# One six-step group becomes two four-step groups, and the whole order of work is written anew

## The chip, the cores and the metric

The kernel runs on one core of a Trainium2 chip. Times are device microseconds of one execution; the time before is the median of three runs. The five engines are TensorE (PE, with its weight loads shown as PEld), VectorE (DVE), ScalarE (ACT), GpSimd (POOL) and SyncE (SP), each with a queue of its own that it works through in the order written; DMAs are issued from the queues of SP, ACT and POOL.

## The reference

A causal convolution over time with three taps and a dilation of 2, a gate, and a projection. With `x` of 2 x 16000 x 256, `w` of 3 x 256 x 512 and `w_o` of 256 x 256, all bf16:

```python
h = x[t] @ w[0] + x[t-2] @ w[1] + x[t-4] @ w[2]      # zero where the time is below 0
f, g = h[..., :256], h[..., 256:]
out = (tanh(f) * sigmoid(g)) @ w_o
```

## The kernel before

**Groups.** Time is cut into groups, listed per sequence in `GROUPS`. A group of kind A has `R` = 256 rows of six consecutive steps (1,536 steps), a group of kind B has `R` rows of four steps. Rows lie on the free axis and channels on the partitions: a transposing DMA from SP loads a group as the tile `xt`. The first group, P160, is computed directly with 320-column matmuls. Since the dilation is 2, even and odd steps don't mix, and a row of six steps is three outputs for each parity, a row of four steps two.

**Fewer products.** Instead of three products per output, an A group makes its three outputs from five products, and a B group its two outputs from four. The operands of the products are sums and differences of shifted views of `xt`; the weights are sums of the taps (`wa`, `wm`, `wp`, and the taps themselves). Each product of a block is two matmuls (two halves of the 256 channels) of 512 columns when R = 256, and of 2R columns in general. A block is one quarter of the 512 output channels of a group, so a group has four blocks, and `ORDER` says in which order blocks are computed.

**The operands.** An A group needs `u1` (for the first product, with `wa`) and four more: `rp` = f + u1, `rm` = e + u1/3, `r0` = u0 - u1/2, `ri` = u2 + 2 u1. The parts `u0`, `u1`, `u2`, `e`, `f` are read from `xt`, by VectorE (whole tiles of 1,024 elements per partition) or by GpSimd (quarters of 256). `u3`, `uh`, `ud` are `u1` times 1/3, -1/2 and 2, made by VectorE. The four sums are mostly made by accumulating DMAs: GpSimd's queue issues a DMA that adds `u1`, `u3`, `uh` or `ud` onto the tile that holds `f`, `e`, `u0` or `u2`, 256 KB each. A B group needs `m`, `p`, `d0`, `d3`, each one difference or sum of views of `xt`.

**The outputs.** The first product goes to PSUM bank `b`; ScalarE copies it to SBUF as `ss`. VectorE combines `ss` and `b` into bank `a`; for A groups a copy `hh` (VectorE or ScalarE) and a second combination `yy` give the middle output. ScalarE applies tanh or sigmoid to `b`, `yy` and `a`. VectorE multiplies the halves (the gate, tile `zz`), TensorE multiplies by `wo_sb` into `o_ps`, ScalarE or VectorE evicts it to `osb`, and SP stores it.

**What sets the order.** `PLAN` is a list of tokens, written by hand or by a planner and executed in that order at build time; each token appends instructions to the queue of its engine. No engine reorders its own queue, and between the queues there are only semaphores for real dependences. The tokens that matter here:

- `F M L Z I`: one product of the next block (first, `rm`, `rp`, `r0`, `ri`; in B blocks F, L, Z, I use `m`, `p`, `d0`, `d3`).
- `P`, `H`, `R`: matmuls of the projection. `c`, `k`, `b`, `y`, `a`, `e`: ScalarE's copies, activations and evictions. `A`, `h`, `Y`, `g`, `v`: VectorE's combinations, gate and evictions.
- `u0.3`: the part u0 of the fourth A group (they count from 0), whole, on VectorE. `u0.3q7`: a quarter of it on GpSimd, held until the VectorE instruction that stands seven places before the latest one is done. `r0.3d`: the accumulating DMA that makes r0 of that group. `rm.2` without the d: the same sum on VectorE.
- `wa.7q2`: a piece of the combined weights on GpSimd.
- `x`: load of the next group on SP. `s9`: a store on SP. A load that stands behind a store on SP waits until that store's evictions are done.

There are four buffers for six-step tiles (the first of them used by group 0) and four for four-step tiles. Groups are numbered in the order of `GROUPS`: 0 is P160, 1 to 8 are the A groups and 9 to 11 the B groups of the first sequence, 12 onward are the second sequence.

The lines that the profile names: L167 load, L325 accumulating DMA, L328 and L330 operands, L359 products, L379 direct convolution, L390 copy `ss`, L393 VectorE's combinations, L403 copy `hh` on ScalarE, L441 activations, L460 gate, L478 projection, L487 and L495 evictions, L504 store.

Of the kernel before, what the change touches and what calls it, by code (L numbers as in the profile page):

```python
# [22 lines left out]
L G c Z g I b f.0 P a L A e0 wa.4q1 P wa.1q1 A F I u1.0 c Z u2.0 a x L b u3.0 Z m.2 I wa.15q1 b F A a wa.12q12 P F  # L23
uh.0 c g Z e1 L e.0 b I e2 A P rm.0d c x F d3.2 a rp.0d L p.2 e3 Z c d0.2 I b P A wa.14q1 a L u2.1 wa.9q27 e4 F A Z
c wa.0q30 I g b wa.8q2 Z a L ud.0 wa.5q10 b I A F wa.2q13 a u1.1 F ri.0d c Z u0.0 c I u3.1 b L r0.0d u0.1 a P A s0 L
wa.11q1 e5 F g wa.13q1 Z c A I wa.10q16 b M f.1 a Z u1.2 k0 P rp.1d b ud.1 F uh.1 L e6 e.1 u0.2q1 F c s3 A I c M
u3.2 u0.2q18 a P Y k1 M rm.1d e.2 e7 Z ri.1d g k2 I L b r0.1d g P a A F e8 uh.2 L u1.3q42 c Y s4 P y s2 A M u1.3q24
x e9 Z h3 u1.3q49 y P Y I b u0.2q39 L v10 a u1.3q47 F Y y u0.2q7 Z c A I r0.2d y P g Z b M u3.3 b F ud.2 k4 f.2 I c
F ud.3 a L u2.2 x c M A P k5 rm.2 P e.3q1 a L Y e11 M A e12 e.3q32 I k6 Z uh.3 e.3q4 Y a P L b ri.2d g I e13 rp.2d F
A y e.3q36 P c v14 Z a Y M b rm.3d P u0.3 k7 Z f.3 y I r0.3d L e.4 b F e15 A f.4q25 F c g P f.4q37 c M a Y P e16 M  # L30
f.4q17 h8 e17 Z f.4q5 h9 y L s8 u1.4q20 I b x A L y u1.4q14 Y F a u1.4q61 Y Z c u1.4q6 I A b M rp.3d u2.3 a F rp.4d
k10 u0.4 Z c ri.3d u2.4 L b P A e18 I ud.4 y M Y F y e.5q66 h11 P c ri.4d Z u3.4 e19 I g rm.4d e20 L a e.5q2 M s9 Y
b P x A P a F k12 g Z c L u1.5 b I uh.4 e21 M A f.5q1 a F y P Y f.5q10 P c h13 f.5q5 Z e22 ud.5 M b u3.5 f.5q1 L h14
y F e23 A I u1.6q79 c P Y s10 a r0.4d L g M e24 Z y e.6q1 A P b h15 P e.5q38 e25 I Y y u1.6q37 F a u2.5 L u1.6q50 Z
c Y P y e.5q42 A M b I e.6q44 v27 e26 F rp.5d k16 g s11 Z c s7 L u0.5 a x I b M A u2.6q18 e28 P h17 F y u1.6q66 Y P
a L uh.5 c I g r0.5d e29 Z e30 e.6q89 M Y b P A a P u2.6q50 h18 e31 F s12 ri.5d P e32 u3.6 u0.6 Z c s13 L y uh.6 x M
rm.5 b I Y e.7q63 k19 F a A L e.6q131 c P A f.7q10 e33 Z M e.7q77 Y b I u2.6q73 h20 y F a f.6 Z c I g L b u2.7q139 M
a A F k21 e.7q134 Y P c L u2.6q7 v34 y M f.7q116 A y P u2.7q105 h22 e35 I Z y rm.6d Y s14 P e36 rp.6d u1.7 I b Z g
r0.6d a F b P u3.7 c ud.6 L u1.8 y ri.6d F A P e38 f.7q79 M c Y I a v37 e.8q153 M e39 Z h23 e.8q119 s15 y P x g b
e.8q1 L a P A k24 F f.7q58 Y P e40 L e.8q86 c v41 Z y ud.7 M A b u0.8q43 P e42 h25 u0.8q134 I e43 F Y u0.8q101 a L  # L40
f.8 e.7q127 c Z I Y y M b A rm.7d P a ud.8 rp.7d F k26 uh.7 Z u0.7 c I g y L r0.7d b M u2.7q72 A P a F k27 u3.8
u2.7q63 P Y e44 L c u1.9 ri.7d s17 I e45 s16 e.9 Z y x M A b P f.9 k28 P Y a F L e46 u2.8 Z e47 g I b u0.9q178 P c A
F e48 uh.8 M u0.9q158 c Y P a u0.9q136 h29 M y Z u0.8q109 h30 s18 I b rm.8d g L a L r0.8d y A F u0.9q4 e49 P Y I c
# [603 lines left out]
```

## Time and profile before

| what | value |
|---|---|
| median of 3 runs | 261.07 us (260.9 to 262.49) |
| profiled execution | 263.16 us |
| its span, first to last instruction | 261.4 us |
| granted TensorE clock over the span | 0.997 |
| busy: PE, DVE, ACT, POOL | 250.4, 244.4, 244.0, 176.2 us |
| matmuls; accumulating DMAs; loads; stores | 1,428; 67; 22; 46 |

An instruction's duration in the profile is longer than the step at which an engine takes the next one, because an engine starts an instruction before the one ahead has drained; the busy time is the union of the intervals. So a matmul of 512 columns is shown with 379 ns while two of them take 0.43 us of the stream, and short waits hide inside the drawn duration.

### The profile page before, as it was taken

The page shows a single profiled execution, that of the slowest core. Times are in us where ns is not written, and L with a number is a line of the kernel's source. Part 1 is how long each engine was busy: PE and PEld are TensorE (multiplying, and loading weights), DVE is VectorE, ACT ScalarE, POOL GpSimd, SP SyncE. Part 2 cuts the span into 40 slices and gives each one's busy share as a digit, 9 for nine tenths or more (in the row PEclk, how much of TensorE's full clock was granted, in tenths as well). Part 3 has the DMA queues.
Part 4 walks back from the last instruction along what each step waited for, and adds up shares of the span by engine and source line. Part 5 has one row for each costly group of instructions (what it writes and reads, how often), then busy time and mean ns, then how long its engine had stood idle before and what let it go on. Part 6 is the DMA issues. An engine that isn't in the chain of part 4 may idle for free.

```text
span 261.4 us, 4573 instructions
## 1 busy us (share of the span) xinstructions
PE 250.4 (96%) x1428; PEld 138.0 (53%) x1428; DVE 244.4 (93%) x405; ACT 244.0 (93%) x490; POOL 176.2 (67%) x248
## 2 busy tenths in 40 slices
PE   8999986999999999999999999999999998999992
PEld 5654543554555645545545555555555554555681
DVE  2899996999999999999999999999999999999963
ACT  5988986999999999999999999999999999989992
POOL 1034884589859668975898798889688878792000
PEclk9999999999999999999999999999999999999998
DMA  6999999998997999999998999899979998275334
GB/s 194 187 208 196 157 154 237 260 203 171 190 242 187 193 203 302 191 219 236 235 268 164 273 195 255 173 215 244 244 146 233 209 227 208 48 182 170 122 128 166
DMA packets 84753, 52.52 MB, mean 201 GB/s; under 512 B 69080, under 2 KB 70360, under 8 KB 84728
## 3 DMA queue, kind: packets, MB, share of 16 engines
q1 hardware_dynamic: 74168, 33.71, 55.1%
q0 software_dynamic: 9648, 17.57, 40.4%
q10 hardware_dynamic: 912, 0.95, 1.1%
q8 instruction: 11, 0.18, 0.3%
q14 instruction: 14, 0.11, 0.1%
HBM read 1.25 MB, written 16.38 MB: 67 GB/s over the span
## 4 chain that ended last, share of the span: by engine, by line
PE 65%; DVE 16%; ACT 8%; issue 4%; DMA 4%; DVEq 0%; ACTq 0%
PE b L359 37%; PE o_ps L478 15%; PE a L359 9%; DVE a L393 5%; DMA u<-uh 4%; DVE zz L460 3%; ACT th L441 2%; ACT sg L441 2%; DVE yy L393 2%; ACT ss L390 2%; DVE u L330 2%; ACT osb L495 2%; PE b L379 1%; PE a L379 1%; PE a L149 1%
## 5 line engine op out<-in xcount | busy, mean ns | idle before, releaser
L478 PE MATMUL o_ps<-wo_sb,zz 128*128 128x256 bf16 x496 | 71.8, 273 | 0.2
L393 DVE SCALAR_TENSOR_TENSOR a<-ss,b 128x512 f32<-128x512 f32 (+1 forms) x88 | 59.6, 679 | 6.4 <-PE b L359 5.7
L495 ACT CAST osb<-o_ps 128x512 bf16<-128x512 f32 x101 | 62.9, 642 | 1.1 <-PE o_ps L478 0.9
L330 POOL TENSOR_TENSOR u<-xt 128x256 bf16<-128x256 bf16 x76 | 55.4, 744 | 11.5 <-PE b L359 7.7
L478 PEld LDWEIGHTS <-zz 128*128 128x128 bf16 x496 | 48.3, 98 | 27.6 <-DVE zz L460 0.8
L390 ACT COPY ss<-b 128x512 f32<-128x512 f32 (+1 forms) x88 | 54.3, 621 | 2.4 <-PE b L359 2.0
L359 PEld LDWEIGHTS <-w_sb 128*128 128x128 bf16 x352 | 34.1, 97 | 38.2 <-issue 3.6
L359 PE MATMUL b<-u,w_sb 128*128 128x512 bf16 x144 | 42.8, 379 | 2.9 <-DMA u<-uh 2.3
L359 PE MATMUL b<-f,wp_sb 128*128 128x512 bf16 x144 | 42.6, 379 | 0.9 <-DMA f<-u 0.7
L359 PE MATMUL a<-u,w_sb 128*128 128x512 bf16 x144 | 42.6, 379 | 0.9 <-DVE a L393 0.8
L359 PE MATMUL b<-u,wa_sb 128*128 128x512 bf16 x144 | 42.6, 379 | 0.4 <-ACT th L441 0.4
L359 PE MATMUL b<-e,wm_sb 128*128 128x512 bf16 x144 | 42.8, 379 | 0.0
L460 DVE TENSOR_TENSOR zz<-th,sg 128x1536 bf16<-128x1536 bf16 (+2 forms) x46 | 41.6, 907 | 0.0
L441 ACT ACTIVATE th<-b 128x512 bf16<-128x512 f32 (+1 forms) x44 | 27.8, 633 | 4.7 <-PE b L359 3.6
L330 POOL TENSOR_TENSOR e<-xt 128x256 bf16<-128x256 bf16 x32 | 25.8, 812 | 6.9 <-DVE a L393 3.4
L330 POOL TENSOR_TENSOR f<-xt 128x256 bf16<-128x256 bf16 x32 | 24.6, 778 | 7.1 <-PE b L359 4.0
L441 ACT ACTIVATE th<-a 128x512 bf16<-128x512 f32 (+1 forms) x44 | 28.0, 637 | 0.4 <-PE a L359 0.3
L441 ACT ACTIVATE sg<-a 128x512 bf16<-128x512 f32 (+1 forms) x44 | 28.0, 637 | 0.0
L441 ACT ACTIVATE sg<-b 128x512 bf16<-128x512 f32 (+1 forms) x44 | 27.7, 629 | 0.3
L393 DVE SCALAR_TENSOR_TENSOR hh<-ss,b 128x512 f32<-128x512 f32 x39 | 26.4, 680 | 0.5 <-PE b L359 0.4
L359 PEld LDWEIGHTS <-wp_sb 128*128 128x128 bf16 x176 | 17.1, 98 | 18.1 <-issue 2.1
L393 DVE SCALAR_TENSOR_TENSOR yy<-hh,b 128x512 f32<-128x512 f32 x39 | 26.3, 680 | 0.1
(68 smaller groups left out, 372.5 us busy)
## 6 DMA issues: line engine op xcount, KB each, us to landing
out_dram<-osb SPq DMA_DIRECT2D x36, 384.0 KB, 3.9
u<-uh POOLq DMA_DIRECT2D x18, 256.0 KB, 4.9
u<-ud POOLq DMA_DIRECT2D x17, 256.0 KB, 6.4
e<-u POOLq DMA_DIRECT2D x16, 256.0 KB, 4.2
f<-u POOLq DMA_DIRECT2D x16, 256.0 KB, 5.7
out_dram<-osb SPq DMA_DIRECT2D x8, 256.0 KB, 5.1
w_sb<-in_w_dram ACTq DMA_DIRECT2D x3, 256.0 KB, 4.1
xt<-in_x_dram SPq DMA_TRANSPOSE x22, 8.6
```

The lines of the kernel that those rows point to most:

```text
L149: nc.tensor.matmul(wps[:], lhsT=ones[:, 0:P], rhs=ones, start=True, stop=True,)
L330: ins = eng.tensor_tensor(out=o, in0=a, in1=b, op=op)
L359: nc.tensor.matmul(G[bank, oi][:, :2 * R], lhsT=wmat[:, ct, osl], rhs=G[mv][:, :, ct, :R], start=which == "first" and ct == 0, stop=ct == ...
L379: nc.tensor.matmul(G[bank, oi][:, :4 * r].rearrange("p (j r) -> p j r", j=4), lhsT=w_taps[tap][:, ct, osl], rhs=xt[:, j0:j0 + 4, ct, c0 + ...
L390: nc.scalar.copy(out=G["ss", oi][:, :n], in_=G["b", oi][:, :n])
L393: return note(nc.vector.scalar_tensor_tensor(out=out, in0=in0, scalar=scalar, in1=in1, op0=ALU.mult, op1=op))
L441: nc.scalar.activation(out=G[name, dt][:, j:j + 2, :R], in_=G[bank, oi][:, :2 * R].rearrange("p (q r) -> p q r", q=2), func=(ACT.Tanh, ACT ...
L460: note(nc.vector.tensor_tensor(out=G["z"][:, dt, :, :n], in0=G["th", dt][:, :, :n], in1=G["sg", dt][:, :, :n], op=ALU.mult))
L478: nc.tensor.matmul(o_ps[:, q, :], lhsT=z, rhs=wo_sb[:, dt, :], start=dt == 0 and (q == 0 or len(dts) == NT), stop=dt == NT - 1, skip_group ...
L495: copy(out=G["osb", at][:, 2 * jp:2 * jp + 2, :], in_=o_ps[:])
```

## The change

Only the three tables `GROUPS`, `ORDER` and `PLAN` change; the functions are the same (every line number is one higher, since one line more stands in `PLAN`). In the second sequence one A group is replaced by a B group of 256 rows at its place near the end of the list and one of 128 rows at the end: 17 A groups and 6 B groups (256, 256, 256, 256, 160, 128 rows) instead of 18 and 4. Groups are numbered anew from there: 12 to 20 are A groups, 21 is the new B group of 256 rows, 22 the one of 160, 23 the one of 128.

In `ORDER` the blocks of group 21 are spread singly among the A blocks of groups 1 to 7, those of group 22 among groups 12 to 18, and group 23 comes last, where 22 stood. `PLAN` is new as a whole: other parts on other engines, 65 accumulating DMAs instead of 67, loads and accumulating DMAs at other places.

```diff
 GROUPS = (
     "P160 A A A A A A A A B B B",
-    "A A A A A A A A A A B160",
+    "A A A A A A A A A B B160 B128",
 )
 ORDER = """
-9 9 9 9 10 10 10 10 11 11 11 11 1 1 1 1 2 2 2 2 3 3 3 3 4 4 4 4 5 5 5 5 6 6 6 6 7 7 7 7 8 8 8 8 12 12 12 12 13 13 13
-13 14 14 14 14 15 15 15 15 16 16 16 16 17 17 17 17 18 18 18 18 19 19 19 19 20 20 20 20 21 21 21 21 22 22 22 22
+9 9 9 9 10 10 10 10 11 11 11 11 1 21 1 1 1 2 2 2 2 3 21 3 3 3 4 4 4 4 5 5 21 5 5 6 6 6 6 7 7 21 7 7 8 8 8 8 12 12 12
+22 12 13 13 13 13 14 14 14 22 14 15 15 15 15 16 16 16 16 22 17 17 17 17 18 18 18 18 22 19 19 19 19 20 20 20 20 23 23
+23 23
 """
 PLAN = """
-d0.0 m.0 d3.0 p.0 F F c G D c D L w L A D wa.7q2 F A wa.3q5 d Z c p.1 Z b d3.1 I b L m.1 a F d0.1 I wa.6q1 c F A a x
...
+d0.0 m.0 p.0 d3.0 F F c G D c D L w L A F wa.4q5 A D wa.1q6 c Z d3.1 I b p.1 Z d F a d0.1 I c m.1 L b L G wa.9q1 x a
...
```

The start of SP's queue before: `xt` are the tiles of loads (128x8x272 a four-step group, 128x12x272 a six-step one), `osb` those of stores.

```order
L167 DMA_TRANSPOSE xt<-in_x_dram 128x8x272
L167 DMA_TRANSPOSE xt<-in_x_dram 128x12x272
L167 DMA_TRANSPOSE xt<-in_x_dram 128x8x272
L167 DMA_TRANSPOSE xt<-in_x_dram 128x12x272 x3
L504 DMA out_dram<-osb_345 128x1024
L504 DMA out_dram<-osb_541 128x1024
L504 DMA out_dram<-osb_624 128x1024
L504 DMA out_dram<-osb_441 128x1024
L167 DMA_TRANSPOSE xt<-in_x_dram 128x12x272 x2
```

And now, from the same load of group 10 on:

```order
L168 DMA_TRANSPOSE xt<-in_x_dram 128x8x272
L168 DMA_TRANSPOSE xt<-in_x_dram 128x12x272
L168 DMA_TRANSPOSE xt<-in_x_dram 128x8x272
L168 DMA_TRANSPOSE xt<-in_x_dram 128x12x272
L168 DMA_TRANSPOSE xt<-in_x_dram 128x8x272
L505 DMA out_dram<-osb_359 128x1024
L168 DMA_TRANSPOSE xt<-in_x_dram 128x12x272
L505 DMA out_dram<-osb_461 128x1024
L505 DMA out_dram<-osb_530 128x1024
L168 DMA_TRANSPOSE xt<-in_x_dram 128x12x272 x3
```

Before, the loads of groups 2, 3 and 4 stood in a row, ahead of any store, and those of 5 and 6 behind four stores. Now the order is 2, 21, a store, 3, two stores, and then 4, 5 and 6 in a row.

The first accumulating DMAs on GpSimd's queue before: `e<-u` makes rm, `f<-u` rp, `u<-ud` ri and `u<-uh` r0; the `wu` and `wa_sb` rows are pieces of the weights.

```order
L325 DMA e<-u_376 128x1024
L325 DMA f<-u_361 128x1024
L233 TENSOR_TENSOR wa_sb<-wu 128x128 x2
L233 TENSOR_TENSOR wu<-wu 128x128
L233 TENSOR_TENSOR wa_sb<-wu 128x128
L233 TENSOR_TENSOR wu<-wu 128x128 x2
L325 DMA u_367<-ud 128x1024
L325 DMA u_514<-uh 128x1024
L233 TENSOR_TENSOR wa_sb<-wu 128x128 x3
L325 DMA f<-u_504 128x1024
```

And now:

```order
L326 DMA u_361<-uh 128x1024
L234 TENSOR_TENSOR wu<-wu 128x128 x2
L326 DMA f<-u_384 128x1024
L326 DMA u_354<-ud 128x1024
L234 TENSOR_TENSOR wu<-wu 128x128
L326 DMA f<-u_542 128x1024
L234 TENSOR_TENSOR wa_sb<-wu 128x128 x3
L234 TENSOR_TENSOR wu<-wu 128x128
L234 TENSOR_TENSOR wa_sb<-wu 128x128 x2
L326 DMA e<-u_625 128x1024
```

The first A group's rm is no longer a DMA (VectorE makes it), its r0 comes first instead of last, and five pieces of `wa_sb` stand between the second group's rp and rm.

More of the change, by code (lines that the diff above doesn't have):

```diff
@@ L27 @@
[L27 to L31, printed above, removed]
@@ new lines @@
+F A wa.7q9 P A c wa.12q5 I g Z P e.0 b P Z u2.0 a L e0 u0.0 F b f.0 I x c F A a L u1.0 c Z e1 g I b L A wa.0q1 P a
+s0 m.2 wa.8q22 Z e2 x F A b I p.2 c Z a u3.0 F d3.2 b L d0.2 I c P A a F e3 uh.0 L rm.0 c r0.0d Z ud.0 I b A L
+wa.3q1 a g P wa.2q21 e4 F A Z rp.0d s2 c m.3 I b ri.0d Z e.1 a L g b wa.6q1 I A F e5 F f.1 c Z a u1.1 L c I d0.3
+rp.1d b P A a M g F wa.14q1 k0 Z c p.3 L wa.10q36 b P A e6 I wa.11q45 d3.3 wa.5q46 F s3 a L x Y e7 P wa.15q7 A c Z
+wa.13q8 e8 u3.1 I u1.2 b M rm.1d Z g k1 F f.2 b I x c uh.1 L u0.1 a F M ud.1 u2.2q1 c A P k2 M u2.1 u2.2q25 a L Y k3
@@ new lines @@
+P e.2q29 y A Z y I r0.1d u3.2 Y L b ri.1d P x a uh.2 ud.2 Z e9 u0.2 F f.3q1 b I A c F u1.3 u2.2q27 e10 M c Y P a
+u2.2q4 h4 Z y M g b I e11 L h5 e.2q1 y F Y e.2q39 L c A P f.3q10 e12 M Y a e.2q68 Z h6 I f.3q14 b A P rm.2d e13 F g
+a rp.2d L c Z u1.4 r0.2d y I u3.3 ri.2d M b Y P k7 A F a P u2.3 e14 L e.3 c e.4q1 Z e15 A P b M u0.3 f.3q70 I e16 Y
+P y F rm.3d h8 e17 Z g c s8 L u0.4q15 a x I Y b P A a L u0.4q82 F y A u0.4q20 Z c v18 e.4q29 I b Z f.4 u0.4q1 y M
+v19 b F e.4q64 h9 P c F rp.3d g a M e20 rp.4d L uh.3 k10 I ud.3 s9 r0.3d A c P s5 e.4q6 a L Y M y ri.3d A I k11 Z
@@ new lines @@
+uh.4 a Y L b P A f.5q24 y Z u1.5 F e21 f.5q6 P b Y I c u3.4 P g e22 rm.4d F y u2.4 M r0.4d c Z g k12 I b M u0.5
+u2.5q84 a L h13 F e23 A P f.5q95 c s10 L f.5q91 s7 Y a P y Y u2.5q96 M e24 Z A e.5q97 k14 I v25 e.5q95 Z b L uh.5 a
+ud.4 F b g ri.4d I c F e.5q93 A e26 M c P s11 h15 e.5q95 a x P Y y M e.6q56 L y h16 e.6q28 Z e27 A u2.5q22 I b L Y
+u2.5q26 a F g y e.6q86 Z c I A P b x M Y a F u3.5 k17 Z ud.5 c v28 L ri.5q79 e29 I A e.6q12 b L y P Y rm.5d F a s12
+f.6 rp.5d Z e30 A r0.5d P c I u1.6 b Z e31 g M rp.6d a I u2.6 b F a P h18 u1.7q58 F c u0.6 L y ri.5q1 M c Y P y
@@ new lines @@
+u1.7q137 A P e32 u1.7q35 M h19 e33 Z s13 e.7q28 h20 y I s1 uh.6 x L b u3.6 P a Y f.7q11 L e34 A ri.5q32 F e35 P Y
+u1.7q79 c Z A ri.5q40 I b P ud.6 rm.6d a u3.7 F g r0.6d y Z s14 c M ri.6d g x P b M k21 u2.7 F y h22 L c u1.8q118 I
+A e36 M u0.7q34 a L Y u1.8q77 e37 P Y y Z u0.7q45 A I e38 e.7q138 P b e.8 e.7q61 Z a F h23 b I f.7q40 c L y g f.7q83
+F M c A P a M e.7q112 h24 e39 x I u0.7q46 Y k25 L v40 a u1.8q62 Z y L A u0.7q53 P e41 Y u1.8q74 P e42 s16 A f.7q122
+I s15 b Z s4 u0.8q23 Y e43 F b rm.7d u3.8 Z ud.7 c I rp.7d u2.8 b F ud.8 a L f.8 u0.8q1 F c A P c M g m.4q20 y Z a M
@@ new lines @@
+h26 ri.7d y I u1.9 L b rp.8d P k27 Y m.4q28 P a A F e44 L uh.7 e45 uh.8 Z r0.7d c A I b f.9q58 P Y a M g F e46
+u0.8q120 Z c h28 I b M f.9q99 e47 L h29 u2.9q130 y F s18 A d3.4q95 P a x f.9q167 L c Y I y u0.8q116 Y P y d0.4q15 A
+Z m.4q89 e48 M ud.9 rm.8d b Z u3.9 r0.8d e49 h30 P s17 F g e50 s6 I c u0.9 s19 L a x P e.9 b M Y p.4q1 e51 P h31
+u2.9q114 P a F A e52 u2.9q97 L c g d3.4q23 Z y P A b I d0.4q135 Y M f.9q59 a F h32 p.4q5 e54 Z m.4q51 c v53 I
+d3.4q62 b L ri.8 u2.10q140 y M A F a p.4q94 h33 P c u2.10q138 P Y y M d3.4q12 e55 g L rm.9d e56 Z p.4q24 Y k34 P I b
@@ new lines @@
+d0.4q10 A L d0.4q46 e57 g rp.9d P a P u2.10q187 y A F Z c u1.10 P u2.9q198 e58 Y I e59 P uh.9 b ri.9d Z u0.10 a
+r0.9d L u3.10 F b f.10 I e61 u1.11q113 A F c P e.10 y I v60 c M rm.10d Z e62 h35 s23 M b P ud.10 a h36 L y F A
+f.11q48 e63 P c Y L s24 u1.11q80 e64 I s22 g rp.10d a x Z y P u1.11q87 A b P Y a M f.11q9 F e66 h37 u2.10q28 Z c I g
+f.11q47 b M y L v65 k38 F u0.11q218 A P a ri.10d Y L c I u1.11q14 A y Z a M Y b P uh.10 Z k39 uh.11 r0.10d F u2.11 b
+L e.11 c F f.12q237 e67 A M c I ud.11 u1.12q122 y h40 P e68 M u0.11q28 Y L a g Z e69 I b Y s26 u0.11q1 P a x A P
@@ new lines @@
+u1.12q31 y F h41 u1.12q94 e70 Z c L u2.12 f.12q99 I b Y M y u1.12q199 A P k42 F s25 u3.11 a Z g rm.11d L c b I
+f.11q61 A e71 P F ud.12 a f.12q213 Y L c P u0.11q89 A e72 Z e.12 rp.11d Z y s27 M u1.13 b r0.11d P b h43 I ri.11d
+e73 F u0.12 a F g c L c I f.13q117 A M e74 M ri.12d e75 h44 I a u3.12 P k45 u2.13q223 Y L y uh.12 P u2.13q5 y A Z a
+L f.12q8 Y b P rm.12d A Z e76 g rp.12d F b Y I r0.12d c F u3.13 a Z e.13 c M g rm.13d b I M k46 u0.13 F y e.14q20
+v77 L k47 P u1.14q37 A c P e79 f.13q21 L Y a M f.13q10 v78 y Z f.13q106 h48 e80 I s29 P b u2.13q21 s28 A L x e81
@@ new lines @@
+u1.14q43 Y P a e.14q95 F Y y Z g c I b P u2.14q12 A M a F rp.13d uh.13 y h49 Z c I g x b u1.14q1 L y M A e82 F h50
+u1.14q118 P a P c Y e.14q143 L e83 v84 e.14q140 M y A I u2.14q112 k51 Z Y u2.13q40 a P b uh.14 r0.13d L s31 u0.14 y
+Z s30 f.15q288 A F s21 b I c P Y u2.14q26 e86 F ud.13 a Z v85 ri.13d c L I b A M u3.14 a F u1.15 k52 Z f.14 I y P g
+b L rp.14d c P u0.15q101 e87 A F M Y c u0.15q112 P k53 M g rm.14d a Z e88 e.15q24 L h54 b I A y e.15q101 P a L Y
+u2.14q137 F e89 A f.15q237 Z c Y I r0.14d b M u2.15 e91 Z uh.15 y F ud.14 P b u1.16 ri.14d I c h55 F f.15q144 a v90
@@ new lines @@
+M c L e.15q36 h56 a s33 M x y e.15q27 A P k57 L f.16q107 Y e92 I Y u0.15q71 Z e93 A P a s32 L b g Z y F A b I c P Y
+e94 F ud.15 M g c ri.15d Z k58 I u3.15 b u2.16 M rm.15d a L h59 f.15q107 e95 F P A y L rp.15d a Y P c f.16q31 P A
+e96 Z y Y s35 I u0.15q54 b s34 L u3.16 d3.5q31 I a u0.16 Z r0.15d F A b P ud.16 e97 e.16 Z F c g I rm.16d b M c
+m.5q3 F e98 h60 M a d3.5q35 v99 P f.16q39 c L h61 m.5q1 a P d3.5q11 e100 A M d0.5q13 y f.16q11 Y L y P A rp.16d k62
+Z g I e102 L b Y I a F uh.16 v101 Z r0.16d c P A b d3.5q12 M ri.16d e103 P h63 y m.5q10 P Y a F L d0.5q15 v104 c
@@ L72 @@
+m.5q3 Z y Y p.5q4 I p.5q3 b A P e105 M g p.5q1 a F s38 h64 P p.5q10 y s37 d0.5q8 Z s36 g c d0.5q11 L b I Y e106 M a
+A F P h65 c Z v108 I b L e107 M Y y P s39 A a F s20 P h66 c I e109 g M e110 L h67 a P Z y A L b Y P y P Y y F I A c
+Z v111 a L v112 Z b I A b v113 F P c g I y Z F a L v114 P b P c A s42 e115 g F s41 L a I s40 c Z A e116 P P a b I
+e117 L Z a A P s43 e118 P v119 b I Z v120 P b P a g s44 e121 P g v122 H e123 H R R s45 e124 v125 s46
 """
```

44 lines of the change are left out of this document (removed).

## The prediction

> **What bounds the kernel now.** First the page's busy times.
>
> ```profile
> span 261.4 us, 4573 instructions
> PE 250.4 (96%) x1428; PEld 138.0 (53%) x1428; DVE 244.4 (93%) x405; ACT 244.0 (93%) x490; POOL 176.2 (67%) x248
> ```
>
> Three engines are nearly full, so the share alone doesn't say which. Next the matmul groups (count, busy, mean ns) and TensorE's timeline where it stood still and at its ends (start, length, instruction, idle before it and releaser).
>
> ```profile
> L359 PE MATMUL b<-u,wa_sb 128*128 128x512 bf16 x144 | 42.6, 379 | 0.4 <-ACT th L441 0.4
> L359 PE MATMUL b<-m,wm_sb 128*128 128x512 bf16 x24 | 6.8, 379 | 0.0
> L359 PE MATMUL b<-m,wm_sb 128*128 128x320 bf16 x8 | 1.7, 299 | 0.0
> L478 PE MATMUL o_ps<-wo_sb,zz 128*128 128x256 bf16 x496 | 71.8, 273 | 0.2
> 0.77 2.72 PE L149 MATMUL a<-const-bfloat16-1.0 128*128 128x512 bf16 x6 [0.77 <-PEq L631]
> 4.83 2.63 PE L379 MATMUL b<-xt,w_sb 128*128 128x320 bf16 x18 [0.16 <-ACT xt L247]
> 35.80 0.59 PE L359 MATMUL b<-u,wa_sb 128*128 128x512 bf16 x2
> 37.13 0.60 PE L359 MATMUL b<-f,wp_sb 128*128 128x512 bf16 x2 [0.74 <-DMA f<-u]
> 37.57 0.59 PE L359 MATMUL b<-u,wa_sb 128*128 128x512 bf16 x2
> 38.00 0.59 PE L359 MATMUL a<-d,w_sb 128*128 128x512 bf16 x2
> 39.30 0.59 PE L359 MATMUL b<-e,wm_sb 128*128 128x512 bf16 x2
> 42.20 0.60 PE L359 MATMUL b<-u,w_sb 128*128 128x512 bf16 x2 [2.30 <-DMA u<-uh]
> 256.10 0.61 PE L478 MATMUL o_ps<-wo_sb,zz 128*128 128x256 bf16 x4
> ```
>
> From 37.57 to 38.00 two 512-column matmuls pass: 216 ns each, 0.42 ns a column. The columns: five products of six-step groups with x144 of 512, four of four-step groups with x24 of 512 and x8 of 320, 500 of 256 for the projection (the row's 496 and 4 of the odd piece), 48 of 320 direct, and 5,632 in warm-up, fill and transposes: 577,024 columns, 243.4 us. From the first matmul (0.77) to the end of the last's stream (256.10 and four at 0.11) are 255.8 us. So 12.4 us are lost between: 2.0 before 4.83 (4.1 us for 4,992 columns), 0.9 before 37.13 and 2.5 before 42.20, both waits for accumulating DMAs, and the remaining 7.0 in small waits. Ahead and behind lie 0.8 and 4.8 us. The drawn lengths hide part of each wait, so the next view, busy time by stretch, shows where the 7.0 lie but not all of it.
>
> ```profile
> 43.00:60.00 17.00, 17.00 (x98) 9.38 (x96) 16.26 (x29) 16.74 (x34) 10.97 (x16) 1.00 1.11 222
> 60.00:100.00 40.00, 39.72 (x222) 21.36 (x220) 39.49 (x65) 39.65 (x80) 31.66 (x46) 1.00 1.04 205
> 100.00:140.00 40.00, 39.26 (x215) 20.62 (x214) 39.86 (x66) 38.72 (x78) 32.53 (x44) 1.00 1.09 231
> 140.00:200.00 60.00, 59.98 (x341) 33.00 (x339) 59.59 (x100) 59.95 (x122) 50.15 (x66) 1.00 1.03 216
> 200.00:250.00 50.00, 48.75 (x284) 27.57 (x283) 48.88 (x78) 48.05 (x97) 32.17 (x47) 1.00 0.72 166
> ```
>
> Columns are the stretch, its length, then PE, PEld, DVE, ACT, POOL. TensorE is idle 1.02 us in 60 to 140, where VectorE has no gap, 0.02 in 140 to 200, 1.25 after. **TensorE's stream is the bound; what is lost on top comes from late DMAs early and from VectorE in the middle.**
>
> **The change, part by part.** *TensorE's work.* A six-step group goes (five products, 8 matmuls of 512 each: 40), two four-step groups come (32 of 512, 32 of 256). The projection stays at 250 row tiles. That is 8 fewer of 512 and 32 more of 256: 4,096 columns, **+1.73 us**, on the path since nothing else bounds the whole. Weight loads of short matmuls cost nothing here: projection matmuls of 256 columns already pass at 0.11 us each.
>
> *VectorE.* Its step per instruction, from the timeline:
>
> ```profile
> 159.96 0.95 DVE L460 TENSOR_TENSOR zz<-th,sg 128x1536 bf16<-128x1536 bf16 x1
> 160.82 0.42 DVE L328 TENSOR_SCALAR ud<-u 128x1024 bf16<-128x1024 bf16 x1
> 161.16 0.68 DVE L330 TENSOR_TENSOR u<-xt 128x1024 bf16<-128x1024 bf16 x1
> 161.76 0.69 DVE L330 TENSOR_TENSOR e<-xt 128x1024 bf16<-128x1024 bf16 x1
> 162.37 0.69 DVE L393 SCALAR_TENSOR_TENSOR a<-ss,b 128x512 f32<-128x512 f32 x1
> 162.97 0.68 DVE L487 CAST osb<-o_ps 128x512 bf16<-128x512 f32 x1
> L393 DVE SCALAR_TENSOR_TENSOR hh<-ss,b 128x512 f32<-128x512 f32 x39 | 26.4, 680 | 0.5 <-PE b L359 0.4
> ```
>
> So 0.86 for a gate of 1,536, 0.34 for a scaling, 0.60 for the rest. By the order's counts: combinations of 512 fall from 195 to 194 (84 and 84 `a`, 39 and 42 `hh`, 72 and 68 `yy`), four of 256 come (0.34 as an estimate), gates go from 36 of 1,536, 6 of 1,024 and 4 of 512 to 34, 8 and 6, scalings from 54 to 51, sums on 1,024 lose one, evictions gain one. In us: -0.6 + 1.4 + 0.1 - 1.0 - 0.6 + 0.6 = -0.1. The total stays; its place changes. A six-step group takes VectorE about 11.5 us (4 `a`, 4 `yy`, 2.2 `hh`, 3.3 sums, 1.3 evictions at 0.60, 2 gates, 3 scalings) against 11.2 of TensorE (40 at 0.216, 24 at 0.108): VectorE can't catch up. A four-step one of 256 rows takes 6.0 (4 `a`, 4 sums, 2 gates at 0.60) against 8.6. Before, such relief stood only at both ends; now one group gives its 2.6 us within groups 1 to 7 and the 160-row one a like amount within 12 to 18. ScalarE gets lighter: `hh` copies fall from 33 to 26, `yy` activations by 4, evictions by 1, against 12 short ones: about 2 us off 244.
>
> Of the 7.0 us of small waits I take 1.8 as gone: the 1.0 idle of 60 to 140, which 140 to 200 shows to be avoidable, and 0.8 for what is hidden in it (each wait is drawn up to 0.16 too short: 0.38 against 0.216). The bounds: 3.9 gone, if all stretches run like 140 to 200; 1.0 more lost, if shorter DMA distances (below) cost what the relief gives.
>
> *The early DMAs.* Accumulating DMAs of three stretches from issue to landing (24 to 41, 41 to 204, 204 to the end), then the one at 24.90 alone, the one at 30.74, those of 38 to 41; then loads of 0 to 26, the one at 26.03, and the later ones; then the queue of SP.
>
> ```profile
> DMA to landing us min/median/max: 5.2/8.5/11.5
> DMA to landing us min/median/max: 3.3/5.4/8.7
> DMA to landing us min/median/max: 3.3/3.8/8.0
> DMA to landing us min/median/max: 5.2/5.2/5.2
> DMA to landing us min/median/max: 9.6/9.6/9.6
> DMA to landing us min/median/max: 7.1/7.9/8.7
> DMA to landing us min/median/max: 4.6/6.6/7.3
> DMA to landing us min/median/max: 14.1/14.1/14.1
> DMA to landing us min/median/max: 5.9/9.2/12.7
> 7.10 26.62 SPq L167 DMA_TRANSPOSE xt<-in_x_dram x6
> 45.65 9.38 SPq L167 DMA_TRANSPOSE xt<-in_x_dram x2
> 25.61 1.19 POOL L325 DMA_DIRECT2D f<-u  x1
> 32.25 0.86 POOL L325 DMA_DIRECT2D u<-uh  x1 [0.65 <-DVE u L330]
> ```
>
> The slow ones stood beside load 4: rp of the first group, issued 0.4 us before that load began, took the 11.5 and caused the first wait; r0, issued at 32.25 while it was still in flight, took 9.9 (32.25 to 42.15) and caused the second. The change issues r0 first, with 10.8 us of TensorE work up to its reader (6.5 before, counted from the order at 216 ns per 512 columns), and puts load 4 behind three stores. **Both waits go.** What is late next: rp of the first group, whose distance falls from 10.8 to 5.6, against 5.2 beside a load in flight: 0.4. Then loads 4, 5, 6 come in a row at about 38 to 54, and r0 and ri of the second group (6.9 each) and the third group's rm (4.8), rp (6.5), r0 and ri (7.8) are issued beside them. With the median 7.9 of those issued at 38 to 41, shortened by the wait before, I take 0.7 for the second group and 0.5 for the third's rm: 1.6 in place of 3.4, **-1.8 us**. Bounds: 0.4, and 5.2 (9.9 - 6.9 and 9.6 - 4.8 - 3.0, the latencies beside load 4, and the 0.4).
>
> Against this speaks a rule of the Trainium skill (page "DMA: Bandwidth & Descriptors", section "Queues, rings and completion order"): each DMA engine alternates between the queues that have work, a packet at a time, so a load in flight would slow an accumulation wherever in the load it is issued, and a distance from its beginning would buy nothing; by it the sum would be that of the first rival below. The rows neither refute nor prove it: 5.2 and 11.5 us both stood beside a load's issue, 0.7 us apart, but the second had a neighbour ahead and a new load behind.
>
> *GpSimd.* Pieces of `wa_sb` now stand between accumulations, the last about 1 us ahead of its reader (1.3 before); GpSimd is 67% busy, so I cost it at nothing; without cover it would be one piece, 0.7. *The end:* the last group has 128 rows instead of 160 and one store instead of two; the same chain of cast, issue and landing remains: 0, within 0.3.
>
> **Sum.** +1.7 - 1.8 - 1.8 = -1.9. The profiled execution took 263.16, 2.1 over the median; the difference is put on the median, 261.07: **259.2 us**.
>
> **The rivals.**
> - *Waits only change place* (chance 0.22). Any load in flight, old or new, slows the accumulations beside it, so that a later load 4 gains nothing; early waits stay at 3.2 and the middle gains 1.0: 261.07 + 1.7 - 0.2 - 1.0 = 261.6. For it: 24 to 41 has a median of 8.5, not one outlier. Against: the median of 5.4 in 41 to 204, though 15 of the 22 loads are issued from 45 on.
> - *VectorE was the whole cause of the small waits* (0.15): they fall to 3.1 and the early ones to 0.4: 261.07 + 1.7 - 3.9 - 3.0 = 255.9. For it: 0.02 idle in 140 to 200. Against: the median distance from an accumulation to its reader falls from 9.1 to 8.0 us.
> - *Three loads in a row* (0.20), slower: load 4 is issued at about 38, 8.6 us of TensorE work ahead of GpSimd's first read of it. If it lands after more than that, as at 14.1 and 12.7 but not at the median of 9.2, GpSimd stands still with the third group's accumulations queued behind, and those run beside load 6: 5.2 early, and short distances cost 1.0 later: 261.07 + 1.7 + 1.8 + 1.0 = 265.6. It decides above some 10 us for load 4.
>
> **How the numbers follow.** The forecast has 0.43, from 257.4 to 260.8. The range reaches to 256.6 below and 264.2 above, which leaves a part of the second and third rival out. About 1% is what a measurement can tell: under 258.5 lie the second rival and a third of the forecast, 0.30; above 263.7 the third, 0.20; the rest, 0.50, between.
>
> **What would show it.** Right: no wait of TensorE over 1 us before 45; waits for DMA of the second and third group under 1 us each; TensorE idle under 0.6 in 60 to 140, with VectorE showing short waits there; matmul columns 581,120. Wrong: GpSimd waiting for load 4 near 47; TensorE waiting for `e<-u` or `u<-uh` at 45 to 55 for more than 2 us; stretches with VectorE full and TensorE idle as before; or a new wait late, where an accumulation has 5 to 6 us to its reader.

## The result and the profile after

| | before | after |
|---|---|---|
| median, both on the same chip | 260.99 us (260.22 to 264.85, 12 runs) | 259.99 us (259.48 to 260.65, 12 runs) |
| profiled execution, its span | 263.16, 261.4 us | 260.08, 258.2 us |
| clock over the span | 0.997 | 0.999 |

The ratio is 0.9958 [0.9941, 0.9974]: 1.0 us faster, 0.4%, inside the 1% that was called no change. The forecast was 259.2, from 256.6 to 264.2.

Of the kernel after, the page's span, busy times and chain of work by engine (before: PE 65%, DVE 16%, ACT 8%, issue 4%, DMA 4%), and a matmul group:

```profile
span 258.2 us, 4610 instructions
PE 251.2 (97%) x1452; PEld 141.0 (55%) x1452; DVE 243.9 (94%) x407; ACT 241.7 (94%) x490; POOL 178.4 (69%) x254
PE 83%; DVE 8%; ACT 4%; issue 2%; POOL 2%; POOLq 0%; DVEq 0%; ACTq 0%
L360 PE MATMUL b<-u,wa_sb 128*128 128x512 bf16 x136 | 40.3, 379 | 0.0
```

Each of the six-step products is down from 144 to 136 matmuls, TensorE has 24 matmuls more, and the chain now runs through TensorE for 83% of its length and through no DMA at all. What TensorE waits for (total us, times, longest):

```profile
PE a L360 <- DVE a L394: 0.8, 1, 0.8
PE a L150 <- PEq L632: 0.8, 1, 0.8
PE a L360 <- DVE hh L394: 0.3, 1, 0.3
PE b L360 <- DVE hh L394: 0.3, 1, 0.3
PE b L360 <- DVE a L394: 0.2, 1, 0.2
```

The `DMA f<-u` and `DMA u<-uh` of before, 0.74 and 2.30 us drawn, have no successor. Busy time by stretch (columns as before: stretch, length, PE, PEld, DVE, ACT, POOL):

```profile
43.00:60.00 17.00, 16.70 (x96) 9.11 (x94) 17.00 (x30) 16.34 (x34) 14.64 (x18) 1.00 1.08 214
60.00:100.00 40.00, 39.77 (x221) 21.40 (x220) 39.25 (x67) 39.67 (x80) 34.47 (x47) 1.00 1.03 223
100.00:140.00 40.00, 39.95 (x225) 21.79 (x224) 39.59 (x64) 39.00 (x79) 36.88 (x53) 1.00 1.10 232
140.00:200.00 60.00, 59.13 (x347) 33.75 (x346) 59.52 (x101) 58.96 (x121) 49.47 (x68) 1.00 0.98 211
200.00:250.00 50.00, 49.64 (x302) 29.06 (x301) 47.97 (x79) 47.98 (x100) 27.90 (x44) 1.00 0.62 150
```

TensorE's idle in 60 to 140 falls from 1.02 to 0.28 us and in 200 to 250 from 1.25 to 0.36, but 140 to 200, which had 0.02, now has 0.87, and 43 to 60, which had none, has 0.30. So the middle is better in sum, and the one long wait has a new place.

The lost time is counted as in the prediction, from one matmul's start to the next less 0.42 ns a column: 12.3 us in the profiled execution before, 7.7 after (2.3 in the head, 5.4 in small waits, none of it early DMA waits). That is 4.6 us, plus 0.3 of a shorter end, less 1.7 for the columns: the 3.2 us between the two spans. The medians differ by a third of that, and the experiments begin there.

### The profile page after: what moved, and what is told of

It reads as the page before. It is cut to its first block, busy times and chain, and to the rows that moved or that the text cites. A ratio compares the mean times of both kernels' runs of the same rounds, so it can differ in the third digit from the quotient of the medians.

```text
span 258.2 us, 4610 instructions
## 1 busy us (share of the span) xinstructions
PE 251.2 (97%) x1452; PEld 141.0 (55%) x1452; DVE 243.9 (94%) x407; ACT 241.7 (94%) x490; POOL 178.4 (69%) x254
## 3 DMA queue, kind: packets, MB, share of 16 engines
HBM read 1.25 MB, written 16.38 MB: 68 GB/s over the span
## 4 chain that ended last, share of the span: by engine, by line
PE 83%; DVE 8%; ACT 4%; issue 2%; POOL 2%; POOLq 0%; DVEq 0%; ACTq 0%
PE b L360 48%; PE o_ps L479 17%; PE a L360 13%; DVE a L394 2%; ACT th L442 1%; PE b L380 1%; DVE zz L461 1%; PE a L380 1%; DVE hh L394 1%; DVE yy L394 1%; PE a L150 1%; DVE f L331 1%; ACT osb L496 1%; ACT sg L442 1%; POOL u L326 1%
## 5 line engine op out<-in xcount | busy, mean ns | idle before, releaser
L394 DVE SCALAR_TENSOR_TENSOR a<-ss,b 128x512 f32<-128x512 f32 (+2 forms) x92 | 61.2, 667 | 2.9 <-PE b L360 2.7
L391 ACT COPY ss<-b 128x512 f32<-128x512 f32 (+2 forms) x92 | 53.8, 588 | 2.7 <-PE b L360 2.1
L331 POOL TENSOR_TENSOR u<-xt 128x256 bf16<-128x256 bf16 x64 | 47.9, 758 | 5.9 <-DVE u L331 1.7
L360 PE MATMUL b<-e,wm_sb 128*128 128x512 bf16 x136 | 40.3, 379 | 0.0
L442 ACT ACTIVATE th<-b 128x512 bf16<-128x512 f32 (+2 forms) x46 | 28.0, 609 | 3.2 <-PE b L360 1.9
L331 POOL TENSOR_TENSOR f<-xt 128x256 bf16<-128x256 bf16 x36 | 29.1, 812 | 2.8 <-PE b L360 2.1
L442 ACT ACTIVATE sg<-b 128x512 bf16<-128x512 f32 (+2 forms) x46 | 28.0, 609 | 1.5 <-PE b L360 1.5
L442 ACT ACTIVATE sg<-a 128x512 bf16<-128x512 f32 (+2 forms) x46 | 28.3, 614 | 0.1
L442 ACT ACTIVATE th<-a 128x512 bf16<-128x512 f32 (+2 forms) x46 | 28.0, 609 | 0.3 <-PE a L360 0.2
L360 PEld LDWEIGHTS <-wm_sb 128*128 128x128 bf16 x184 | 18.0, 98 | 14.9 <-issue 0.6
```

The costliest lines, as they stand in the source:

```text
L331: ins = eng.tensor_tensor(out=o, in0=a, in1=b, op=op)
L360: nc.tensor.matmul(G[bank, oi][:, :2 * R], lhsT=wmat[:, ct, osl], rhs=G[mv][:, :, ct, :R], start=which == "first" and ct == 0, stop=ct == ...
L391: nc.scalar.copy(out=G["ss", oi][:, :n], in_=G["b", oi][:, :n])
L394: return note(nc.vector.scalar_tensor_tensor(out=out, in0=in0, scalar=scalar, in1=in1, op0=ALU.mult, op1=op))
L442: nc.scalar.activation(out=G[name, dt][:, j:j + 2, :R], in_=G[bank, oi][:, :2 * R].rearrange("p (q r) -> p q r", q=2), func=(ACT.Tanh, ACT ...
```

## The experiments

The expectations come first; "before" and "after" are the two kernels, and where no other is named, a median is compared with that of before, run on the same chip in the same set.

### Before and after, profiled once more

Nothing is edited in these two.

> The kernel before, unchanged, profiled again. Theory 1 (the two early waits of TensorE belong to this order of instructions): they come again, 3.4 us lost between 35 and 43 us, span 259 to 262. Rival (the profiled execution of before, 2.1 us over its median, was an unlucky one): rp of the first group lands within 8 us, the waits are under 1.5 us together, and the span is 258 to 260, so that most of the 3.2 us between the two spans was the draw and not the change.

> The changed kernel, unchanged, profiled again. Theory 1: no wait of TensorE over 0.6 us before 45 us, span 257.6 to 258.8, the largest single waits again at 146 and 202 us. Rival (small waits are drawn anew in every execution): the places of the waits over 0.4 us differ, the sum being the same within 1 us.

Before took 260.59 us, span 258.8. TensorE's waits in this second execution of before:

```profile
PE a L359 <- DVE a L393: 0.8, 1, 0.8
PE a L149 <- PEq L631: 0.8, 1, 0.8
PE b L359 <- ACT th L441: 0.4, 1, 0.4
PE b L359 <- DVE yy L393: 0.3, 2, 0.2
PE a L359 <- DMA u<-ud: 0.3, 1, 0.3
```

Its busy time by stretch:

```profile
60.00:100.00 40.00, 39.79 (x221) 21.41 (x221) 39.49 (x67) 39.66 (x80) 31.78 (x45) 1.00 1.05 221
100.00:140.00 40.00, 38.95 (x214) 20.59 (x213) 39.65 (x66) 38.41 (x77) 32.38 (x43) 1.00 1.00 211
140.00:200.00 60.00, 59.98 (x337) 32.68 (x336) 59.60 (x100) 59.92 (x122) 50.14 (x68) 1.00 1.08 221
200.00:250.00 50.00, 48.76 (x292) 28.33 (x291) 47.60 (x75) 48.08 (x98) 29.64 (x43) 1.00 0.66 156
```

The two early waits are gone without any change: 3.4 us belonged to the execution first profiled, not to the kernel. Lost are 9.8 us in place of 12.3. rp of the first group landed after 8.9 us, later than the rival had set (8), and still in time. The later waits stand at the same matmuls with the same sizes within 0.05 us, some 2.9 us earlier up to a new DMA wait at 122 us (the `u<-ud` above, 0.5 from matmul to matmul) and 2.6 from there on: they belong to the kernel.

After took 264.85 us, span 263.0, clock 0.993. TensorE's longest wait in this execution:

```profile
PE a L360 <- DMA u<-ud: 3.3, 1, 3.3
```

The DMA that it waits for, among those issued within 46.3 to 46.6 (the last figure is the time to landing):

```profile
u<-ud POOLq DMA_DIRECT2D x1, 256.0 KB, 10.8
```

TensorE's timeline around it (start, length):

```profile
53.38 0.59 PE L360 MATMUL b<-u,w_sb 128*128 128x512 bf16 x2
57.28 0.59 PE L360 MATMUL a<-u,w_sb 128*128 128x512 bf16 x2 [3.31 <-DMA u<-ud]
57.71 0.72 PE L479 MATMUL o_ps<-wo_sb,zz 128*128 128x256 bf16 x4
58.22 1.06 PE L360 MATMUL b<-u,wa_sb 128*128 128x512 bf16 x2
```

And the stretch behind it, where the third column from the end is the granted clock:

```profile
57.00:60.50 3.50, 3.22 (x12) 1.50 (x12) 1.18 (x3) 1.71 (x3) 1.16 (x2) 0.65 1.16 222
```

So after can have such a wait too. It was ri of the second group, issued at 46.44; load 6 began 0.25 us later, and the sum took 10.8 us. In the first profile of after that load began 1.41 us behind the same sum, which took 5.9 (issued at 46.70) and came 1.4 us before its reader. Then the wait costs a second time: from 58.22 on each matmul of 512 columns takes 0.43 instead of 0.22 us for about 3 us, at a granted clock of 0.65 in that stretch, some 1.7 us more.

### Distance at one place, given and taken

In before, load 4 is put behind the store `s3`:

```diff
-... A P rm.0d c x F d3.2 ...     ... F c s3 A I ...
+... A P rm.0d c F d3.2 ...       ... F c s3 x A I ...
```

> The kernel before, with the load of group 4 on SP moved behind the first two stores (one token moved), so that no load begins beside the first group's accumulating DMAs. Theory 1 (that load made them late): rp and r0 of the first group land within 6 us, the two early waits fall to under 0.7 us together, and the time falls by 0.5 to 2.5 us. Rival (VectorE, or any load in flight, sets the pace there): the waits move a little and the time stays within 0.5 us.

268.19 us (266.75 to 269.39), ratio 1.0272 [1.024, 1.0303]: 7 us slower where a gain was expected. The first group's sums did become fast, 3.3 to 5.2 us, but load 4 now began at 37.65 and stood in this kernel's chain of work (start, length):

```profile
37.65 10.61 DMA xt<-in_x_dram
```

From its timeline, GpSimd's, VectorE's and TensorE's next instructions on that path (start, length, idle before and releaser):

```profile
48.42 3.64 POOL L329 TENSOR_TENSOR u<-xt 128x256 bf16<-128x256 bf16 x6 [6.85 <-PE a L358]
...
51.52 0.83 DVE L327 TENSOR_SCALAR u<-u 128x1024 bf16<-128x1024 bf16 x1 [4.64 <-POOL u L329]
...
56.07 1.01 PE L358 MATMUL a<-u,w_sb 128*128 128x512 bf16 x2 [4.74 <-DVE yy L392]
```

GpSimd, next in line to read the new tile, stood 6.85 us; VectorE waited for GpSimd's quarters and TensorE for VectorE; and the half rate followed here as well. The releaser drawn for GpSimd is a matmul, long done; the load landed at 48.26. This is the rival "Three loads in a row", in an order that has no slack for a late load 4.

A milder distance in before: `s2` and load 4 behind the eviction `e4`.

```diff
-... wa.9q27 e4 F A Z c ...
+... wa.9q27 e4 s2 x F A Z c ...
```

> The kernel before, with the store of the first half of group 9 moved on SP ahead of the load of group 4, so that this load begins at about 28.5 us, 2.5 us behind the issue of the first group's rp and 2 us ahead of its ri. Theory (an accumulating DMA is late when a load begins within half a microsecond of its issue): rp lands within 6 us; the early waits go; the median falls by 0.3 to 0.8 us, to the level of the executions of before without early waits. Rival (any load in flight does it): ri and r0 of the first group become late instead, waits of 1 us or more before 43 us, the median not lower. GpSimd's first read of group 4 stays ahead of its need, unlike where the load began at 37.65.

260.86 us (260.02 to 262.78), ratio 1.0003 [0.9982, 1.0025]. Load 4 began at 28.97, the early sums took 3.9 to 5.3 us, and no early wait is left; its longest waits:

```profile
PE a L359 <- DMA u<-ud: 1.1, 1, 1.1
PE a L359 <- DVE a L393: 0.8, 1, 0.8
```

The first ends at 226.2. Its sum took 5.3 us instead of the 3.9 of the first profile of before, and between its issue (220.9) and its landing the trace has no packet of a load: what made it late is open. So the distance alone, without the new groups, brought nothing that the median shows.

In after, the distance is undone: load 4 directly behind load 3.

```diff
-... Z e2 x F A b ...       ... F s3 a L x Y e7 ...
+... Z e2 x x F A b ...     ... F s3 a L Y e7 ...
```

> The changed kernel, with the load of group 4 moved back ahead of the stores, right behind that of group 3, so that it begins beside r0 and rp of the first group. Theory 1: rp takes 8 us or more, TensorE waits 1.5 to 4 us before 45 us, and the time rises by 1 to 3 us over the changed kernel, to 261 to 263. Rival (r0 first in the queue and longer distances made the difference, not the load): the waits stay under 0.7 us and the time within 0.5 us of 260.0.

261.43 us (259.93 to 263.92), 1.4 us over the median of after; ratio to before 1.0011 [0.9989, 1.0034]. Load 4 began at 28.71. TensorE's longest wait, and then the sums issued in 28 to 32.5 with their times to landing:

```profile
PE b L359 <- DMA f<-u: 2.4, 1, 2.4
```

```profile
u<-uh POOLq DMA_DIRECT2D x1, 256.0 KB, 8.9
f<-u POOLq DMA_DIRECT2D x1, 256.0 KB, 8.1
u<-ud POOLq DMA_DIRECT2D x1, 256.0 KB, 9.3
```

In after they took 4.1, 4.0 and 4.8. The profiled execution (262.41) lies 1.0 us over the median of this kernel, so its wait is a draw too; by the medians the distance pays here: with after's short way from rp to its reader, a load beside the first sums costs the whole gain.

### VectorE's room, from both sides

In each kernel one scaling more for every six-step group, its result not used, so the output is the same:

```diff
+junk = wh_sb[:].rearrange("p ct d -> p (ct d)")
 ...
 note(pre(*group_of(token), nc.vector))
+if token.startswith("uh."):
+    nc.vector.tensor_scalar_mul(junk, groups[group_of(token)[0]]["u1"].rearrange("p q ct r -> p (q ct r)"), 1.0)
```

> The kernel before, with one more VectorE scaling (0.34 us) for each of the 18 six-step groups, 6.0 us in all; its result is written to a tile that nobody reads any more. Theory (in the order of before VectorE has no room among the six-step groups): most of it lengthens the kernel, +4 to +6 us, 264.5 to 267. Rival (the small waits have other causes and VectorE has room): under +2 us.

> The changed kernel with the same extra scaling for each of its 17 six-step groups, 5.7 us in all. Theory (the two four-step groups spread among the six-step ones give VectorE some 5 us of room): +0.5 to +2.5 us over 260.0, at least 2 us less than the same addition costs before. Rival (VectorE's total is the same in both kernels, so is its room): as much as before, within 1 us.

Before went to 268.40 (ratio 1.0291 [1.0266, 1.0316]), 7.5 us for 6.1 of work, after to 268.41 (1.0285 [1.0265, 1.0305]), 8.4 us over its own 260.0 for 5.8. The stretch with the blocks of the 160-row group, in before with the addition and then in after with it:

```profile
140.00:200.00 60.00, 58.72 (x333) 32.31 (x332) 59.68 (x102) 59.13 (x119) 50.69 (x65) 1.00 1.00 206
```

```profile
140.00:200.00 60.00, 56.17 (x323) 31.43 (x322) 59.66 (x98) 55.73 (x113) 48.89 (x67) 1.00 0.94 193
```

TensorE's idle there goes from 0.02 to 1.28 us in before, from 0.87 to 3.83 in after. The spread groups were to give VectorE room; they gave none that could be filled, and the rival of the second run (as much as before, within 1 us) was right.

The other way: the scaling of u1 by 1/3 is left out in each six-step group, and the middle product's sum adds u1 itself, so the middle outputs are other numbers.

```diff
+elif token.startswith("u3."):
+    G = groups[group_of(token)[0]]
+    G["u3"] = G["u1"]
+    made_v.append(made_v[-1])
```

> The changed kernel without the scaling of u1 by 1/3 in each of its 17 six-step groups: the sum for the middle product adds u1 itself, so the middle outputs are other numbers; VectorE does 17 x 0.34 = 5.8 us less. Theory 1 (the small waits are VectorE's queue, which has no room): they shrink by most of what VectorE saves, so the time falls by 3.5 to 5.5 us from 260.0, to 254.5 to 256.5, and the small waits from 5.3 to under 2 us. Rival (they are chains of single results between ScalarE, VectorE and TensorE, fixed by the order, which a shorter VectorE queue does not touch): it falls by less than 2 us, to 258 or above. Adding 5.7 us had cost 8.4 us.

> The kernel before without the scaling of u1 by 1/3 in each of its 18 six-step groups (the sum for the middle product adds u1 itself, so the middle outputs are other numbers): VectorE does 18 x 0.34 = 6.1 us less. Theory 1 (the small waits are VectorE's queue): the time falls by 5 to 7 us from 261.0, to 254 to 256, more than in the changed kernel since it had 7.6 us of small waits against 5.3, and by the columns (577,024 against 581,120) it then ends up to 1.7 us below the changed kernel without these scalings: the change's gain was to take VectorE's waits away, and without them it costs its 1.7 us. Rival (chains of single results): it falls by under 2 us and stays above the changed kernel without them.

After without them: 258.62 (257.9 to 262.25, four runs), ratio 0.9907 [0.988, 0.9934], 1.4 us under after; the run at 262.25 stands alone, and the median of the other three is 258.18, 1.8 under. Before without them: 259.59 (259.09 to 261.35), 0.9957 [0.9936, 0.9979], 1.5 us under the before of that set (261.08). The busy times on the page of after without them, and on that of before without them:

```profile
PE 250.9 (98%) x1452; PEld 141.2 (55%) x1452; DVE 239.9 (93%) x390; ACT 241.3 (94%) x490; POOL 176.0 (68%) x254
```

```profile
PE 250.1 (97%) x1428; PEld 138.6 (54%) x1428; DVE 239.3 (93%) x387; ACT 243.4 (94%) x490; POOL 175.2 (68%) x248
```

Counted as above, the lost time falls only from 7.7 to 6.7 in after and from 9.8 (second execution) to 8.3 in before. Some 6 us less of VectorE give 1.4 to 1.8 in after and 1.5 in before, 6 us more cost 7.5 to 8.4: VectorE has no room for more, and little of what is lost now goes with its work. The forecast of the rival was right in both runs; that the remaining waits are chains of single results, as it has it, is not shown by that. The second half of the first theory fell with it: without the scalings after stays 1.0 us or more ahead of before, so its advantage doesn't rest on a VectorE that is short.

### The longest wait of after, and a version with both mends

After's longest wait, from its timeline: VectorE's sum `f` of group 14 took 1.38 us beside GpSimd's, where 0.69 is usual, and the combination `a` behind it, of the 160-row group, came late.

```profile
145.61 1.38 DVE L331 TENSOR_TENSOR f<-xt 128x1024 bf16<-128x1024 bf16 x1
145.82 1.63 POOL L331 TENSOR_TENSOR u<-xt 128x256 bf16<-128x256 bf16 x1
...
146.91 0.48 DVE L394 SCALAR_TENSOR_TENSOR a<-ss,b 128x320 f32<-128x320 f32 x1
...
147.44 0.43 PE L360 MATMUL a<-d,w_sb 128*128 128x320 bf16 x2 [0.84 <-DVE a L394]
```

The two are swapped, and then, in a second kernel, load 6 is also put behind the store `s5` and the eviction `e10`:

```diff
-... F b f.10 I e61 u1.11q113 A F ...     ... L b ri.1d P x a uh.2 ...   ... u2.2q27 e10 M c ...
+... F b A f.10 I e61 u1.11q113 F ...     ... L b ri.1d P a uh.2 ...     ... u2.2q27 e10 s5 x M c ...
```

> The changed kernel, with one combination (of the first block of group 22, before the wait of 0.84 us at 147 us) moved one VectorE instruction earlier, ahead of the sum f that took 1.38 us there. Theory (the small waits are fixed by the order, and this one by a single late VectorE instruction): the wait goes, span and median fall by 0.6 to 1.0 us, to 259.0 to 259.4. Rival (VectorE has no room there and the next instruction is late instead): within 0.3 us of the changed kernel.

> The changed kernel with the swap of the run before (the first group of 320 columns makes its `a` ahead of `f.10`), and with the store `s5` and the sixth `x` behind it moved to right behind the eviction `e10`. Theory 1 (an accumulation issued just before a load begins is the slow one): in the changed kernel's slow execution ri of the second group was issued 0.25 us before load 6 began and took 10.8 us; here load 6 begins about 1.9 us after it, so ri lands in under 7 us in every execution and the slow ones (261 to 265 us) go: no run above 261, median 259.5 to 259.8, beside 259.74 for the swap alone. Rival (any load in flight slows them, the distance from its beginning buys nothing): ri or another sum of the second and third group still takes over 8 us, and runs above 261 stay as frequent as in the changed kernel.

The swap gives 259.74 (259.54 to 260.48), ratio to before 0.9955 [0.9937, 0.9972]. The wait of 0.84 went, and another of the same size came a block later, as the rival had it (`f` now 0.99 and the next sum `e` 1.11 us beside GpSimd):

```profile
PE b L359 <- DVE hh L393: 1.1, 2, 0.8
PE a L149 <- PEq L631: 0.8, 1, 0.8
```

With load 6 later: 259.84 (259.61 to 260.51, 12 runs), 0.9962 [0.9943, 0.9982]. ri of the second group took 4.9 us (load 6 began 3.05 us behind its issue) and came 2.5 us before its reader instead of 1.4. No run was above 261, but none of the 12 timed runs of after was either, so that the rare wait is gone isn't shown. By the medians both versions are level with after.

## Why the prediction was right, and where its size was off

**The columns: right.** 581,120 are there, +1.73 us, paid in full.

**Small waits: the size about right, the reason not shown.** 1.8 us were taken as gone. Between the executions without an early wait, the second of before and the first of after, the lost time falls from 9.76 to 7.74: 2.0 us, of which 0.5 are the DMA wait at 122 us in that execution of before. They went from 60 to 140 (1.26 us idle there in that execution of before, 0.28 after), as said, and from 200 to 250, which was not said; 140 to 200 and 43 to 60 got worse. The reason given was VectorE's relief, read from stretches of before: no gap of VectorE in 60 to 140, where TensorE waited. But those rows show 0.51 and 0.14 us of its idle there, and 0.41 in 140 to 200, where TensorE didn't wait, so they don't set the stretches apart. Against the reason speak also the runs with more and with less of VectorE: both kernels answer almost alike, in both directions. What remains is that the new order has fewer places where a single result comes late. No run has isolated that, and none has tried ScalarE, which is 2.3 us lighter in after (244.0 to 241.7).

**Early DMA waits: the step that failed, by its size.** The prediction put 3.4 us of waits to the kernel and 1.6 in their place, -1.8; and the 2.1 us by which the profiled execution lay over the median it put on the median as a difference of level. Those 2.1 us were mostly these waits. The second execution of before has neither, nor the 2.1. What their removal is worth in the median is about what is left over: the two executions without them differ by 0.6 in span (+1.7 - 2.0 - 0.3, the last from the end), the medians by 1.0, so 0.4. That is a remainder and no measurement of its own; with the interval of the ratio, 0.7 to 1.5 us for the 1.0, it is 0.1 to 0.9. And the run with the milder distance in before shows no gain, within -0.5 and +0.7 us by its interval. With 1.8 for a term that is worth some 0.4 the forecast came out too low, 0.8 under the median.

**The mechanism of that step: right in after, weaker in before.** r0 of the first group, 9.9 us in the first profile of before, takes 4.1 in the first of after, and beside load 4 again 8.9, with rp at 8.1 and 1.4 us lost in the median. In before the same order gave both: in the second execution load 4 began 0.82 us ahead of rp's issue instead of 0.42 behind it, rp took 8.9 us instead of 11.5 and r0 5.2 instead of 9.9, and neither was waited for. Against the mechanism stood the rule of the Trainium skill (page "DMA: Bandwidth & Descriptors", section "Queues, rings and completion order") that engines alternate between queues packet by packet; from it the prediction drew that distance from a load's beginning buys nothing. One sum, ri of the second group, tells: with load 6 beginning 0.25, 1.41 and 3.05 us behind its issue it took 10.8, 5.9 and 4.9. If the turns were equal, a sum that takes 3.3 us alone (the shortest here) would take some 6.4 beside a load from 0.25 us on, as an estimate; the measured 10.8 is more. The rule alone doesn't give these numbers. The rate of the DMA engines tells more. Four stretches follow: rp, ri and r0 beside load 4 in before, ri beside load 6 in the second execution of after, and from the first execution of after one in which only packets of loads start and one in which only those of sums move data (the last figure is GB/s, the one before it the busy share of the DMA engines):

```profile
30.50:36.50 6.00, 5.89 (x32) 2.84 (x29) 6.00 (x12) 5.68 (x12) 4.42 (x7) 1.00 1.32 84
50.50:54.50 4.00, 3.19 (x16) 1.46 (x15) 4.00 (x8) 3.45 (x8) 3.02 (x6) 1.00 1.28 88
47.50:49.00 1.50, 1.50 (x8) 0.61 (x7) 1.50 (x4) 1.50 (x4) 1.40 (x2) 1.00 1.27 290
49.50:51.50 2.00, 2.00 (x13) 1.03 (x11) 2.00 (x4) 2.00 (x5) 1.28 (x2) 1.00 1.17 210
```

Where packets of a load and of sums mix, the two together move 84 to 88 GB/s with the engines busy throughout; where they follow each other, 290 and 210. So these late sums didn't share a full rate with a load: both crawled. What makes the two mix in one execution and follow each other in another is open.

**The rivals.** "Waits only change place" (261.6) held in one thing, the new wait in 140 to 200; of its early waits of 3.2 us the first profiled execution of after has none, the second has one of 3.3. "VectorE was the whole cause" fell with the two runs with less of it. "Three loads in a row" didn't decide: load 4 was issued at 38.80 and landed after 8.4 us, under the point of some 10, and GpSimd stood nowhere for it. In before with load 4 behind `s3` it took 10.6 us, and the collapse came as described. And something close to a listed sign against the forecast, a wait over 2 us for `e<-u` or `u<-uh` at 45 to 55, occurred in one of the two profiled executions of after, beside load 6: 3.3 us for `u<-ud` of the second group, up to 57.3.

## What to carry to other kernels

A wait for a DMA in one profiled execution is one draw: profile again before it goes into a sum, and where that execution lies over the median by about the size of its waits, take the waits to be that difference. A load begun right beside a short transfer that something waits for can double its latency (4.1 to 8.9 us, 4.9 to 10.8); moving the load cost nothing here where its own reader had slack, and much more than it saved where it had none. Where two engines are both nearly full, more work on the second shows that it has no room, but only less work on it shows whether it costs anything now.

## What the hardware showed unexpectedly

**A wait of over 3 us is paid again.** After waits of 3.5 and 4.9 us from matmul to matmul TensorE ran for about 3 us at half rate: the stretch's clock was 0.65 behind the first, and 0.52 behind the second (56 to 59.5 in before with load 4 behind `s3`), 1.6 to 1.7 us more each. Behind the 2.4 us wait of after with the early load 4 the clock of the span was 1.0. The Trainium skill (page "TensorE: Matmul & The Clock Gate", section "What's actually happening") gives a window of about 3.4 us of activity after which the clock is halved or restored; these rows agree with it: the stretch from 58.05 to 61.46 in the second execution of after, 3.41 us long, is granted 0.50.

**Waits repeat to a few hundredths of a microsecond.** Apart from DMA waits, the same matmuls waited for the same results in both profiled executions of each kernel: the one behind `f` lost 1.01 and 1.00 us in the two of after, the next largest 0.49 and 0.48. In these four profiles a wait on an engine belonged to the order, one on a DMA to the execution.

**One sum on VectorE cost double.** 1.38 instead of 0.69 us while GpSimd made a quarter of another, and 0.99 and 1.11 for two sums after the swap. That GpSimd's work is the cause is not shown: a sum at 143.07 in after took 0.74 while GpSimd made a quarter too.
